# A searched table of steps: loads, transposes, dummies and output queues of a fused attention and gMLP kernel set in a new order

## The chip, the cores and the metric

The kernel runs on one core of a Trainium2 chip. The metric is the device time of one execution in microseconds (us). Engines are named as the profile names them: PE is the matrix engine (PEld its weight loads), DVE the vector engine, ACT the scalar engine, POOL GpSimd, SP the engine that issues most of the DMAs.

## The reference

One row of conditioning `c` is turned into six vectors, and these modulate a linear attention (hedgehog features, 16 heads of 28) and a gMLP with a 2048 x 2048 spatial matrix, over x of 2048 rows x 448.

```python
mod = (silu(c) @ w_mod)            # sa, ca, ga, sb, cb, gb, 448 each
# stage A
h = layernorm(x) * (1 + ca) + sa
q, k, v = split(h @ wqkv)          # 16 heads of 28
phi_q = concat(softmax(q @ w_phi), softmax(-q @ w_phi))
phi_k = concat(softmax(k @ w_phi), softmax(-k @ w_phi))
kv = sum_s phi_k^T v ;  z = sum_s phi_k
o = (phi_q @ kv) / (phi_q . z + 1e-6)
x = x + ga * (o @ wo)
# stage B
h = layernorm(x) * (1 + cb) + sb
z1, z2 = split(gelu(h @ w_in))     # 896 each
g = w_sp @ layernorm(z2) + b_sp    # w_sp 2048 x 2048, over the rows
x = x + gb * ((z1 * g) @ w_out)
```

## The kernel before

The 2048 rows are 16 tiles of 128, numbered 0 to 15. The work is cut into some 970 steps, and the string `ORDER` (lines 482 to 535) is the program: `fast_path` walks its words one after the other and issues what each names. Every engine runs its own instructions in that order and waits, by semaphores, for what it needs; nothing is reordered at run time. A word reads like this:

```python
kM:14@3      # step kM of tile 14, result in PSUM bank 3
kP:14/V      # step kP of tile 14, on DVE (/S is ACT, /G POOL, /Y SP)
ld:wout/Y    # load of w_out, issued by SP
T1:14,16     # DMA transpose of tiles 14 and 15, always on SP
```

The steps that the change and the prediction speak of, in order of the program:

- **Start.** `du:n` (L734) is n dummy matmuls on a zero tile, with no result. `ct` (L745) turns the row c; `FT`/`ET` (L824, L828) transpose the raw q and k weights, `PF`/`EP` (L840, L828) fold w_phi into them; `csA`/`ccA`, `csB`/`ccB` (L769) make the modulation vectors of stage A and stage B; `SH` (L783) and `SC` put them into the weights. `X:0` to `X:3` (L871) transpose the first four tiles of layernormed x on PE.
- **Stage 1, the keys.** Tiles 4 to 15 of layernormed x are transposed by DMA, two tiles a time: `T1:a,b` (issued at L863, `f_hT<-f_xpad`). Then, per tile, `kM` (L881) projects the keys, `kE`/`kF` (L884) take the exponentials on ACT, `kS` (L895), `kR` (L899) and `kP` (L902) normalise them, `vM` (L889) and `vC` project the values, and `kA` (L912) adds the tile to the sums kv, 8 small matmuls in one PSUM slot for all 16 tiles. `qM:0` to `qM:7` (L929) with `qE`/`qF` make the query features, each for four tiles and half of the heads. `gr:0` (L940) needs the load `wmga` and makes the gate ga, `gr:1` needs `wmgb` and makes gb. `kA:15` ends stage 1; `KV` copies the sums.
- **Stage 2, attention out and the input of the MLP.** `nM` (L957) multiplies query features by the sums, `nC`, `nS`, `nV`, `nT`, `nA` divide (`nT` is L976, on DVE), `T2` (L863, `f_oo<-f_oo`) transposes by DMA, `wM` (L992) multiplies by wo; `wN` is `wM` with one more matmul (L990) that adds x on PE. `wR`, `wQ`, `l2r`, `l2a` are the second layernorm, `T3` (L1032, `f_hT<-f_xpad`) its DMA transpose. `zM` (L1038) and `yM` (L1068) are the two halves of h @ w_in. `W:t,u` (L1076) loads an eighth of a quarter of w_sp by DMA transpose, 256 KB.
- **Spatial product and output.** `pM` (L1148) multiplies by w_sp, `oM` (L1097) by w_out, `oE` (L1113) adds to x, `oD` (L1116) stores a tile. Tile 15 is done in two halves, `oH`, `oG`, `oF` (L1102, L1106, L1110).

The loads go to SP in the order of their words (L655 to L686), with the transposes T1, T2, T3 and W between them, so one queue carries nearly all transfers. A DMA takes one of eight semaphores in turn, so the issue of a DMA on a queue waits for the landing of the one eight places earlier that used it. A function `general_path` stands behind a flag and isn't run with these inputs.

Of the kernel before, what the change touches and what calls it, by code (L numbers as in the profile page):

```python
# [486 lines left out]
SCq:2/S SCq:3/S SCq:0/S scb l1a:2/G X:2@6 XE:2/V ld:wv/Y ld:x4/Y SHv@2 SCv:2/V SCv:3/V l1e:4,8/G l1r:4,8 l1a:4/G SCv:0/S l1a:6/G kM:0@4 kM:1@7 kF:1
l1a:5/G SCv:1/S kE:1 kE:0 kF:0 kM:2@5 qM:0@A1 kE:2 qF:0 qE:0 ld:wmga/Y l1s:8 l1s:10 l1s:9 gr:0@0 ld:x5/Y ld:wo/Y kF:2 ge:0 vM:3@6 vM:1@4 vC:1 W:0,0
l1a:7/G m4 T1:4,6 kS:1 ld:wmgb/Y l1s:11 kS:0 kR:1 l1e:8,12/G kR:0 l1s:13 kP:1/G l1r:8,12 l1a:11/G T1:6,8 vM:0@7 l1s:12 kP:0/V kS:2 kR:2 W:0,5
ld:win1/Y l1a:9/G vM:2@3 vC:2 vC:0 l1s:14 l1s:15 l1e:12,16/G kM:3@5 kE:3 vC:3 l1r:12,16 l1a:15/G l1a:8/V T1:8,10 l1a:10/G kP:2/V T1:10,12 kM:5@2  # L490
kM:4@3 l1a:12/G l1a:14/G m6 kF:3 ld:wsb/Y T1:14,16 wos:3/V kS:3 kA:0@A0 l1a:13/G T1:12,14 kF:4 kR:3 kP:3/V kF:5 kE:5 kS:5 kE:4 W:0,3 W:0,6 kS:4 kR:4
vM:4@4 qM:1@C qF:1 kM:6@5 kF:6 kE:6 qM:2@A1 kS:6 qE:1 kP:4/V kR:5 qF:2 vM:5@5 vC:4 kA:1@A0 vC:5 kA:2@A0 kA:3@A0 qE:2 kM:7@7 kE:7 kF:7 ld:wcb/Y
ld:win0/Y wos:2/G kR:6 kP:5/V vM:7@4 vC:7 kS:7 kR:7 kP:7/V kM:8@6 kF:8 kE:8 kS:8 gr:1@7 W:0,4 kP:6/G kR:8 vM:6@5 kM:9@2 kE:9 kM:11@4 kF:9 kM:10@6 ge:1
kS:9 wos:1/G kR:9 kA:4@A0 kA:5@A0 vC:6 kA:6@A0 kE:11 kA:7@A0 kE:10 kF:10 kF:11 kS:11 kP:8/G kS:10 kR:10 kP:10/V vM:8@5 vC:8 vM:9@4 vC:9 kM:12@2 kE:12
kF:12 kA:8@A0 kM:14@3 kM:13@5 kP:9/G kE:13 kR:11 kP:11/G kS:12 kR:12 kF:13 ld:wout/Y kS:13 kR:13 kE:14 W:0,2 kM:15@7 kF:14 vM:10@2 vC:10 kA:9@A0 kF:15
kE:15 vM:13@6 vC:13 W:0,1 kP:12/V kS:14 kA:10@A0 vM:11@4 vC:11 vM:12@7 vC:12 vM:14@2 vC:14 kP:13/G kA:11@A0 kA:12@A0 vM:15@5 vC:15 kS:15 kR:15
kA:13@A0 kR:14 kP:14/V kA:14@A0 wts:1/G kP:15/V kA:15@A0 KV:1 qM:3@C qE:3 KV:0 csB@3 esB ccB@4 ecB nM:0@A1 nX:0 qF:3 nC:0 YB@1 YE W:0,7 nM:1@A2
wos:0/G wts:5/G wts:4/G SCw:1,0/G nX:1 nC:1 nS:0 nV:0 nT:0 nA:0/G T2:0,1 nT:1 nA:1/V T2:1,2 SCw:2,0/S SHw:2@0 SCw:0,2/S qM:4@C qF:4 nM:2@A0 nX:2
SHw:3@3 SCw:0,3/V nC:2 SCw:3,1/G qE:4 nM:3@A2 nX:3 SCw:2,1/S SCw:1,1/S qM:5@A1 qE:5 nM:4@C W:1,1 nC:3 nS:1 nV:1 nT:3 nT:2 nM:5@A2 nX:5 wN:0@0 nC:5
wN:1@1 nX:4 nC:4 nS:2 qF:5 wR:0/S wts:0/G wR:1/S nA:2/V nA:3/G T2:2,4 nV:2 nT:5 nA:5/G nT:4 W:1,3 nM:7@A1 nX:7 nC:7 wQ:0/S nM:6@A2 nX:6 qM:6@A0 wQ:1/S  # L500
lA:0,2/G lB:0,2/G lC:0,2/G lD:0,2/G SCw:3,0/S qF:6 nA:4/V T2:4,6 nC:6 nS:3 nV:3 nT:6 W:1,7 qE:6 wM:3@6 wN:2@7 wR:2/S l2r:0,2 l2a:1/G T3:1,2 nT:7
wR:3/V wQ:3/S qM:7@A2 qE:7 qF:7 nA:7/V l2a:0/G lA:2,4/G lB:2,4/G T3:0,1 wM:4@7 wQ:2/V lC:2,4/V lD:2,4/V l2r:2,4 l2a:2/G wR:4/V nA:6/V T2:6,8 l2a:3/G
# [803 lines left out]
```

## Time and profile before

| what | value |
| --- | --- |
| median of 3 runs | 250.22 us (249.93 to 250.77) |
| the profiled execution | 250.54 us, its span 248.7 us |
| mean granted PE clock | 0.995 |
| PE busy | 239.2 us, 96% of the span |
| DVE busy | 187.5 us, 75% |
| ACT busy | 115.7 us, 47% |
| POOL busy | 128.3 us, 52% |
| DMA, mean over the span | 25.23 MB, 101 GB/s |

Times in the views are counted from the start of the span. "Busy" of PE counts pipelined matmuls whose ends are modelled, so 96% says that PE has nearly no gap, not that it is at its peak. A row of a timeline gives start, length, engine, line, operation, output and inputs, count, and in brackets the idle time just before it with what ended it. Rows of SP in a timeline are the issue of a DMA, and that includes the time in which SP waited for room in the ring of semaphores; the time to landing is in the rows of the DMA view.

### The profile page before, as it was taken

What the parts mean: (1) busy time and instruction counts of PE and PEld (TensorE: products, weight loads), DVE (VectorE), ACT (ScalarE), POOL (GpSimd) and SP (SyncE); (2) the same over time, 40 slices, a digit from 0 to 9 for tenths busy, and PEclk for the clock granted to TensorE, in tenths of its full rate; (3) what the DMA queues carried; (4) which work ended last, traced back from release to release, by engine and by line L of the source; (5) the groups of instructions that cost most, each with busy time, mean ns of one, the idle gap of its engine ahead of it and who ended that gap; (6) DMA issues with size and microseconds to landing.
All of it is one profiled execution on the core that took longest, in us unless ns stands there. A gap on an engine that the chain in (4) does not pass through costs nothing.

```text
span 248.7 us, 4220 instructions
## 1 busy us (share of the span) xinstructions
PE 239.2 (96%) x1520; PEld 127.2 (51%) x1528; DVE 187.5 (75%) x374; ACT 115.7 (47%) x231; POOL 128.3 (52%) x172
## 2 busy tenths in 40 slices
PE   8899999999889999999999999999999999999992
PEld 6755566566535555544444444444444544444652
DVE  2889998977988988967357985858899754727652
ACT  3999887738889888787878110000010000000000
POOL 4768878576678556747855449601541901401000
PEclk9999999999999999999999999999999999999998
DMA  7998989970595634782100960009930120000022
GB/s 190 307 279 166 206 171 234 204 191 0 100 167 115 128 88 86 168 154 60 42 0 4 152 102 0 3 0 155 187 79 3 55 74 0 3 0 3 18 78 86
DMA packets 68800, 25.23 MB, mean 101 GB/s; under 512 B 58401, under 2 KB 68642, under 8 KB 68770
## 3 DMA queue, kind: packets, MB, share of 16 engines
q1 hardware_dynamic: 68160, 24.41, 48.9%
q10 hardware_dynamic: 610, 0.46, 0.6%
q8 instruction: 14, 0.23, 0.4%
q14 instruction: 16, 0.13, 0.2%
HBM read 8.87 MB, written 1.84 MB: 43 GB/s over the span
## 4 chain that ended last, share of the span: by engine, by line
PE 81%; DVE 10%; ACT 4%; DMA 2%; issue 1%; DVEq 0%; ACTq 0%; SPq 0%
PE f_psum L1148 29%; PE f_psum L1068 10%; PE f_psum L1038 9%; PE f_psum L1097 8%; PE f_psum L1084 6%; PE f_psum L992 4%; PE f_psum L929 3%; PE f_psum L881 3%; DVE f_ksum L895 2%; PE f_psum L889 2%; DVE f_t L976 2%; DMA f_oo<-f_oo 2%; PE f_psum L734 2%; DVE f_phik L902 1%; PE f_psum L957 1%; PE f_psum L783 1%
## 5 line engine op out<-in xcount | busy, mean ns | idle before, releaser
L1148 PEld LDWEIGHTS <-f_z2n 128*128 128x128 bf16 x192 | 18.7, 98 | 22.4
L1148 PE MATMUL f_psum<-f_wsp,f_z2n 128*128 128x512 bf16 x119 | 27.1, 379 | 0.1
L1068 PE MATMUL f_psum<-f_hT,f_win 112*128 112x512 bf16 x112 | 26.3, 379 | 0.0
L1038 PE MATMUL f_psum<-f_win,f_hT 112*128 112x448 bf16 (+1 forms) x128 | 26.1, 352 | 0.0
L1148 PE MATMUL f_psum<-f_hT,f_Eq 128*128 128x512 bf16 x92 | 22.3, 379 | 0.2
L1168 ACT COPY f_Eq<-f_psum 128x512 f32<-128x512 f32 x4 | 2.3, 586 | 40.0 <-PE f_psum L1148 40.0
L1097 PE MATMUL f_psum<-f_wout,f_z1T 128*128 128x448 bf16 x105 | 20.4, 352 | 0.0
L1071 ACT ACTIVATE f_z1T<-f_psum,f_yb 128x512 bf16<-128x512 f32 x28 | 17.8, 686 | 3.3 <-PE f_psum L1068 3.3
L934 ACT ACTIVATE f_Eq<-f_psum 112x1024 bf16<-112x1024 f32 x16 | 16.1, 1037 | 5.1 <-PE f_psum L929 5.1
L1038 PEld LDWEIGHTS <-f_hT 112*128 112x128 bf16 (+1 forms) x128 | 12.3, 97 | 11.7 <-DVE f_t L976 0.2
L1200 POOL TENSOR_TENSOR f_z1T<-f_gb,f_z1T 128x512 bf16<-128x512 f32 x6 | 7.8, 1310 | 19.3 <-DVE f_gb L1175 19.3
L976 DVE TENSOR_TENSOR f_t<-f_psum,f_w 128x896 bf16<-128x896 f32 x16 | 16.9, 1086 | 0.5
L895 DVE TENSOR_REDUCE f_ksum<-f_E 128x32 f32<-128x896 bf16 x16 | 16.8, 1066 | 0.6 <-ACT f_E L884 0.5
L1068 PEld LDWEIGHTS <-f_win 112*128 112x128 bf16 x112 | 10.9, 98 | 12.2
L884 ACT ACTIVATE f_E<-f_psum 128x448 bf16<-128x448 f32 x32 | 15.7, 565 | 2.6 <-PE f_psum L881 2.5
L1042 ACT ACTIVATE f_z2g<-f_psum 128x896 bf16<-128x896 f32 x16 | 14.6, 915 | 4.9 <-PE f_psum L1038 3.5
L929 PE MATMUL f_psum<-f_hT,f_Wq 113*128 113x512 bf16 (+1 forms) x64 | 15.2, 378 | 0.0
L1148 PEld LDWEIGHTS <-f_Eq 128*128 128x128 bf16 x96 | 9.4, 98 | 11.3
L992 PE MATMUL f_psum<-f_win,f_oo 112*128 112x448 bf16 x64 | 14.1, 352 | 1.1 <-DMA f_oo<-f_oo 0.9
L1097 PEld LDWEIGHTS <-f_z1T 128*128 128x128 bf16 x105 | 10.2, 98 | 9.4
L1113 DVE TENSOR_TENSOR f_xpad<-f_psum,f_x 128x448 bf16<-128x448 f32 x15 | 9.0, 618 | 7.5 <-PE f_psum L1097 7.5
L1175 DVE TENSOR_TENSOR f_z2g<-f_psum,f_z2g 128x512 f32<-128x512 f32 x12 | 8.3, 688 | 8.4 <-PE f_psum L1148 8.0
(214 smaller groups left out, 513.5 us busy)
## 6 DMA issues: line engine op xcount, KB each, us to landing
out_dram<-f_xpad SPq DMA_DIRECT2D x15, 112.0 KB, 1.7
f_wm<-in_w_mod_dram SPq DMA_DIRECT2D x4, 406.0 KB, 5.0
f_win<-in_B_w_in_dram SPq DMA_DIRECT2D x2, 784.0 KB, 6.6
f_x<-in_A_x_dram SPq DMA_DIRECT2D x3, 448.0 KB, 8.3
f_wmg<-in_w_mod_dram SPq DMA_DIRECT2D x2, 392.0 KB, 7.2
f_wout<-in_B_w_out_dram SPq DMA_DIRECT2D x1, 784.0 KB, 9.2
f_bsp<-in_B_b_sp_dram SPq DMA_DIRECT2D x1, 512.0 KB
f_wq_raw<-in_A_wqkv_dram ACTq DMA_DIRECT2D x1, 392.0 KB, 3.9
```

The costliest lines, as they stand in the source:

```text
L884: nc.scalar.activation(out=Er[i % NR][:, s, :], in_=ps["k" + str(i)][:, 0, 0:D], func=ACT.Exp, scale=1.0 - 2.0 * s)
L895: nc.vector.tensor_reduce(out=ksum[:, i], in_=Er[i % NR][:].rearrange("p s (c f h) -> p (s c) h f", c=4, h=HP), axis=AX.X, op=ALU.add)
L929: nc.tensor.matmul(t[:, u, :], lhsT=Wq[0:KR[m], m, cc * CB:cc * CB + P], rhs=hT[0:KR[m], 4 * st:4 * st + 4, m, :], start=(m == 0), stop=(m ...
L934: nc.scalar.activation(out=Eq[st // 2][0:CB, 2 * c2:2 * c2 + 2, s, (st % 2) * 512:(st % 2 + 1) * 512], in_=ps["q" + str(n)][0:CB, :, :], f ...
L976: nc.vector.tensor_tensor(out=tr[i % 2][:], in0=numv(i)[:, :, :, 0:DH], in1=wr[i // 2 % 2][:, i % 2].unsqueeze(3).to_broadcast([P, 2, H, D ...
L992: nc.tensor.matmul(t[:, 0, 0:D], lhsT=oT[0:CB, i % 4, cc, :], rhs=wo_s[0:CB, cc, :], start=(cc == 0 and not with_x), stop=(cc == KC - 1))
L1038: nc.tensor.matmul(t[:, hf, 0:D], lhsT=hT[0:KR[m], i, m, :], rhs=win_s[0:KR[m], m, FH + hf * D:FH + (hf + 1) * D], start=(m == 0), stop=(m ...
L1068: nc.tensor.matmul(t[:, 0, :], lhsT=win_s[0:CB, m, fc * P:(fc + 1) * P], rhs=hT[0:CB, 4 * st:4 * st + 4, m, :], start=(m == 0), stop=(m == ...
L1071: nc.scalar.activation(out=stage_b()["z1T"][:, fc, st * 512:(st + 1) * 512], in_=ps["y%d_%d" % (st, fc)][:, 0, :], func=ACT.Gelu_apprx_tan ...
L1084: nc.tensor.matmul(g[:, 0, 0:b - a], lhsT=later["z2n"][:, s_, fc * P:(fc + 1) * P], rhs=wspT[t][:, s_, a:b], start=(s_ == 0), stop=(s_ == ...
L1097: nc.tensor.matmul(ps["o" + str(t)][:, 0, 0:D], lhsT=later["z1T"][:, fc, t * P:(t + 1) * P], rhs=wout_s[:, fc, :], start=(fc == 0), stop=( ...
L1148: nc.tensor.matmul(t[:, 0, :], lhsT=b[:, j, f * P:(f + 1) * P], rhs=a[:, j, :], start=(PSTART[k] and j == 0), stop=(j == NH - 1), skip_gro ...
```

## The change

Only the string `ORDER` differs; no step has new code. The table has 975 words in place of 973:

- The dummies are 9, then five groups of 3 (24 matmuls), in place of 18, 3, 6 and 6 (33).
- The loads at the start stand in another order: on SP x0, phi, wk, x1 in place of x1, wk, phi, x2, x0; on ACT's queue c ahead of wq.
- Behind the first twelve loads of SP, the loads, the transposes T1 and the W loads are mixed in another order (below).
- `wN:2` is `wM:2`: the matmul that adds x in tile 2 goes (tiles 0 and 1 keep it), and DVE adds x there.
- Some 80 steps run on another engine than before (`kP` of 0, 1, 6 and others between POOL and DVE, `EP`, `SC`, `wQ` and `nA` between ACT, DVE and POOL).
- PE's own steps stand in another order within stages 1 and 2 and the start.
- Outputs: `oD` of tiles 1, 7, 8, 13 and 14 are issued by ACT in place of SP; of the two halves of tile 15 one changes from SP to ACT and the other from ACT to SP: `oF:15,0` is on ACT now, `oF:15,1` on SP.

Two lines of the string, the first words and the last:

```diff
-ld:wq/S m3 m2b/G m1/V m2a/G du:18@0 du:3@5 ld:c/S ct@2 tbl ce:1 ce:2 m5 ld:x1/Y l1s:1 ce:3 l1e:1,2/V l1r:1,2 l1a:1/G FTq:1@5 ETq:1/S FTq:0@6 ETq:0/S
+du:9@2 ld:x0/Y l1s:0 m1/V m5 du:3@3 ld:c/S ct@0 du:3@3 ld:wq/S FTq:1@5 m2a/G m2b/G l1e:0,1/G l1r:0,1 l1a:0/G m4 tbl ce:1 ce:2 ce:3 ce:4 ld:phi/Y bd/V
...
-oM:12,0,7@3 oE:12 oM:13,0,7@2 oE:13 oD:7/Y oD:10/Y oD:11/Y oD:9/Y oD:13/Y oD:12/Y oM:14,0,7@1 oE:14 oD:14/Y oH:15,0@5 oG:15,0 oF:15,0/Y oH:15,1@6
-oG:15,1 oF:15,1/S hint
+oM:12,0,7@3 oM:13,0,7@2 oE:13 oD:13/S oD:2/Y oE:12 oD:12/Y oE:10 oD:11/Y oD:10/Y oM:14,0,7@1 oE:14 oD:14/S oH:15,0@5 oG:15,0 oF:15,0/S oH:15,1@6
+oG:15,1 hint oF:15,1/Y
```

**SP in stage 1.** Before, these rows stand on SP behind the loads of x and of wo (L863 into `f_hT` is T1, L1076 is W, L681 the load wmgb, L662 the loads wsb and then wcb, L655 into `f_win` from `in_B_w_in` is win1 and then win0):

```order
L1076 DMA_TRANSPOSE f_wsp_84<-in_B_w_sp_dram 128x8x128
L863 DMA_TRANSPOSE f_hT<-f_xpad 128x8x128
L681 DMA f_wmg<-in_w_mod_dram 112x4x448
L863 DMA_TRANSPOSE f_hT<-f_xpad 128x8x128
L1076 DMA_TRANSPOSE f_wsp_84<-in_B_w_sp_dram 128x8x128
L655 DMA f_win<-in_B_w_in_dram 112x4x896
L863 DMA_TRANSPOSE f_hT<-f_xpad 128x8x128 x2
L662 DMA f_wm_120<-in_w_mod_dram 112x4x464
L863 DMA_TRANSPOSE f_hT<-f_xpad 128x8x128 x2
```

After, these rows stand behind the loads of x (L685 is wout, L655 from `in_A_wo` is wo, L686 is bsp; of the six T1 the first is T1:4,6, then T1:6,8 and T1:10,12, then T1:8,10 and T1:12,14, the last T1:14,16):

```order
L1076 DMA_TRANSPOSE f_wsp_84<-in_B_w_sp_dram 128x8x128
L685 DMA f_wout<-in_B_w_out_dram 128x7x448
L863 DMA_TRANSPOSE f_hT<-f_xpad 128x8x128
L655 DMA f_win<-in_A_wo_dram 112x4x448
L681 DMA f_wmg<-in_w_mod_dram 112x4x448
L662 DMA f_wm_120<-in_w_mod_dram 112x4x464
L863 DMA_TRANSPOSE f_hT<-f_xpad 128x8x128 x2
L1076 DMA_TRANSPOSE f_wsp_84<-in_B_w_sp_dram 128x8x128 x3
L863 DMA_TRANSPOSE f_hT<-f_xpad 128x8x128 x2
L1076 DMA_TRANSPOSE f_wsp_84<-in_B_w_sp_dram 128x8x128
L662 DMA f_wm_120<-in_w_mod_dram 112x4x464
L1076 DMA_TRANSPOSE f_wsp_84<-in_B_w_sp_dram 128x8x128
```

and directly behind them:

```order
L655 DMA f_win<-in_B_w_in_dram 112x4x896
L686 DMA f_bsp<-in_B_b_sp_dram 128x2048
L863 DMA_TRANSPOSE f_hT<-f_xpad 128x8x128
L1076 DMA_TRANSPOSE f_wsp_84<-in_B_w_sp_dram 128x8x128
L655 DMA f_win<-in_B_w_in_dram 112x4x896
```

Before, two W and one half of w_in stood ahead of the T1:14,16 (the first of the last pair, T1:12,14 is the second). After, T1:14,16 is the last of the six and stands behind six W, wout, one half of w_in, both L662 loads and bsp, which before stood behind T3:10,12, deep in stage 2.

**PE behind the first three tiles of keys.** Before, the queries of the first four tiles (L929) follow:

```order
L881 MATMUL f_psum<-f_Wk,f_hT 128x448
L881 LDWEIGHTS f_hT
L881 MATMUL f_psum<-f_Wk,f_hT 128x448
L929 LDWEIGHTS f_Wq
L929 MATMUL f_psum<-f_hT,f_Wq 128x512
```

After, the gate's matmuls (L940, `gr:0`) follow at that place, and `qM:0` comes behind three `vM`:

```order
L881 MATMUL f_psum<-f_Wk,f_hT 128x448
L881 LDWEIGHTS f_hT
L881 MATMUL f_psum<-f_Wk,f_hT 128x448
L940 LDWEIGHTS f_scb
L940 MATMUL f_psum<-f_wmg,f_scb 128x448
```

So `gr:0` stands 8 matmuls of 512 columns earlier than before.

**Outputs on SP.** The rows at the end of SP's program before (L1218 reads the flag of the general path):

```order
L1116 DMA out_dram<-f_xpad 128x448 x8
L1218 TENSOR_LOAD flag
L1218 ISA x2
L1116 DMA out_dram<-f_xpad 128x448 x7
L1110 DMA out_dram<-f_xpad 128x224
```

and after:

```order
L1116 DMA out_dram<-f_xpad 128x448 x6
L1218 TENSOR_LOAD flag
L1218 ISA x2
L1116 DMA out_dram<-f_xpad 128x448 x4
L1110 DMA out_dram<-f_xpad 128x224
```

Five full outputs and the first half of tile 15 are issued by ACT now, and the second half, the last, by SP.

More of the change, by code (lines that the diff above doesn't have):

```diff
@@ L487 @@
[L487 to L502, printed above, removed]
@@ L535 @@
+cA:1,1,12 cX:1,1,12/V gG:2,6 oM:8,0,7@3 oE:8 oD:8/S oM:9,0,7@2 oE:9 oD:9/Y cX:1,1,22/V gM:4,6@6 oM:10,0,7@0 gG:3,6 gG:4,6 read oM:11,0,7@4 oE:11
+oM:12,0,7@3 oM:13,0,7@2 oE:13 oD:13/S oD:2/Y oE:12 oD:12/Y oE:10 oD:11/Y oD:10/Y oM:14,0,7@1 oE:14 oD:14/S oH:15,0@5 oG:15,0 oF:15,0/S oH:15,1@6
+oG:15,1 hint oF:15,1/Y
 """
```

81 lines of the change are left out of this document (48 added, 33 removed).

## The prediction

> **What bounds the kernel now.** I read the page first: its busy times, its slices, its chain.
>
> ```profile
> span 248.7 us, 4220 instructions
> PE 239.2 (96%) x1520; PEld 127.2 (51%) x1528; DVE 187.5 (75%) x374; ACT 115.7 (47%) x231; POOL 128.3 (52%) x172
> PE   8899999999889999999999999999999999999992
> DMA  7998989970595634782100960009930120000022
> ```
>
> PE is busy for 239.2 us of 248.7, and its row has only nines behind the second slice, but for slices 11 and 12 (62 to 75 us) and the last. So the time is the start of steady PE work, plus PE's work, plus what it waits, plus the tail. The second thing to see is the DMA row: 7 to 9 tenths in the first nine slices, up to 56 us. The transfers of stage 1 are nearly as full as PE there, and they feed it. PE's timeline gives the start of the steady part, the end of stage 1 and all later waits:
>
> ```profile
> 15.55 2.45 PE L881 MATMUL f_psum<-f_Wk,f_hT 113*128 113x448 bf16 x12
> 53.59 1.90 PE L929 MATMUL f_psum<-f_hT,f_Wq 113*128 113x512 bf16 x8
> 64.74 0.59 PE L957 MATMUL f_psum<-f_KVbd,f_Eq 112*128 112x120 bf16 x8 [0.67 <-DVE f_t L976]
> 65.73 0.35 PE L990 MATMUL f_psum<-f_x,f_ident 128*128 128x448 bf16 x1 [0.40 <-DVE f_t L976]
> 71.38 0.93 PE L992 MATMUL f_psum<-f_win,f_oo 112*128 112x448 bf16 x4 [0.89 <-DMA f_oo<-f_oo]
> 80.58 1.67 PE L992 MATMUL f_psum<-f_win,f_oo 112*128 112x448 bf16 x8 [0.20 <-DVE f_t L976]
> ```
>
> The first keys (kM) start at 15.55; `kA:15` has ended and `qM:3` starts at 53.59. Call that point K. Between them no row shows a wait. The four waits in stage 2 add up to 2.16 us, and that is all there is to be gained behind the start, except for the tail.
>
> **The main term: T1:14,16.** The last transpose of layernormed x is now issued behind much more. Before:
>
> ```profile
> 33.17 3.68 SPq L863 DMA_TRANSPOSE f_hT<-f_xpad  x2
> f_hT<-f_xpad SPq DMA_TRANSPOSE x1, 5.3
> 42.32 0.58 SPq L685 DMA_DIRECT2D f_wout<-in_B_w_out_dram  x1
> f_wout<-in_B_w_out_dram SPq DMA_DIRECT2D x1, 784.0 KB, 9.2
> f_win<-in_B_w_in_dram SPq DMA_DIRECT2D x2, 784.0 KB, 6.6
> f_bsp<-in_B_b_sp_dram SPq DMA_DIRECT2D x1, 512.0 KB
> ```
>
> The first row's first transfer is T1:14,16; the second row is its time from issue to landing, so it landed at 33.17 + 5.3 = 38.5. Where will it land? I count what stands ahead of it in the new order: behind the loads of x these are wo, wmgb, wsb, wcb, win1, wout, bsp, six W and the other five T1. Compare what before had issued when it came to wout, at 42.32: the same loads without bsp and with win0, five W, and six T1. A W is 128x8x128 in bf16, 256 KB, and so is a T1. The new set, with T1:14,16 itself, has one W and bsp more (768 KB) and one half of w_in less (784 KB): equal to 16 KB. Before, that set had landed with wout, at 42.32 + 9.2 = 51.5. So with the queue as full as before, T1:14,16 would land at 51.5 in place of 38.5.
>
> The queue can be fuller, since before it had holes:
>
> ```profile
> 6.00:18.00 12.00, 11.09 (x140) 8.26 (x138) 10.70 (x35) 11.55 (x22) 8.14 (x14) 1.00 1.14 303
> 18.00:22.00 4.00, 4.00 (x22) 1.95 (x20) 3.83 (x9) 4.00 (x8) 3.10 (x9) 1.00 1.19 103
> 30.00:35.00 5.00, 5.00 (x45) 3.10 (x44) 4.97 (x7) 5.00 (x10) 4.56 (x8) 1.00 0.63 109
> 35.00:46.70 11.70, 11.70 (x94) 7.04 (x93) 10.69 (x19) 8.59 (x20) 7.92 (x5) 1.00 1.13 237
> ```
>
> The last column is GB/s. Full, with loads and transposes mixed, it moved 237. In 18 to 22 it moved 103, so 4 x (1 - 103/237) = 2.3 us went unused; in 30 to 35, 5 x (1 - 109/237) = 2.7. In the new order wout stands in the first hole, where SP waited for tiles 4 and 5 of layernormed x. All 5.0 recovered gives 46.5, none gives 51.5; new holes at transposes that wait for x can open too. I take 3.2 of the 5.0, so 48.3.
>
> When does PE need it? Prices of its steps, from the chain of waits:
>
> ```profile
> 33.24 0.76 PE f_psum L881 x4
> 34.00 0.76 PE f_psum L889 x4
> 29.50 1.74 PE f_psum L929 x8
> 25.82 0.42 PE f_psum L912 x8
> 55.49 0.78 PE f_psum L769 x32
> ```
>
> In the new order, from its first kM to `kM:14`, stand 14 kM, 12 vM and 2 gates (28 x 0.76 = 21.3), 3 qM (5.2) and 10 kA (4.2): 30.7 us. From 15.5 that is 46.2. So PE waits 2.1 there. From `kM:14` to the end of `kA:15` stand 2 kM, 4 vM, 6 kA and csB (half of the last row), 7.5 us, and DVE and POOL have kS, kR and kP of the last two tiles to do meanwhile. K becomes 48.3 + 0.1 + 7.5 = 55.9 in place of 53.59: **+2.3** (0 to +5.5 for landings of 46.2 to 51.5; the first 7.7 us of the delay, 38.5 to 46.2, cost nothing). An earlier wait costs nothing beside it: T1:6,8 stands behind wout and wsb now (1.2 MB, some 5 us at 237) and may keep `kM:7` 1 to 2 us, but then `kM:14` is reached later and its wait is shorter by as much.
>
> [...]
>
> **The start.**
>
> ```profile
> 1.23 3.85 PE L734 MATMUL f_psum<-f_zero 128*128 128x256 bf16 x21 [1.23 <-DVE f_zero L695]
> 6.17 0.82 PE L734 MATMUL f_psum<-f_zero 128*128 128x256 bf16 x6
> f_wmg<-in_w_mod_dram SPq DMA_DIRECT2D x1, 392.0 KB, 10.6
> 7.05 1.20 SPq L680 DMA_DIRECT2D f_wmg<-in_w_mod_dram  x1
> ```
>
> The dummies fill time in which PE waits for the first weights, so nine fewer take nothing off by themselves. The weights' chain through ACT is one step shorter (an `EP` on DVE); the first kM can be up to 0.5 earlier. But `gr:0` now follows the first three kM, near 17.3, and its load landed at 7.05 + 10.6 = 17.6, so PE waits there for 0.3 to 0.8. Together **0** (-0.5 to +0.8).
>
> **Stage 2.** The matmul that adds x in tile 2 goes (about 0.2 where it is not at a gap, and DVE adds x as for other tiles), and csB moves ahead of K (about 0.4, counted there). Its waits have other places: T2 now stands behind fewer loads but between other W, and `nT` on DVE (L976) still paces `nM`. I can't read from the trace which of the four waits go; I see new places of equal size (`yM:0,0` behind T3:2,4, `zM:11` right behind `zM:12` in one PSUM slot). All four gone would be -2.2 and new ones of their size +2.2. As the nearest rows are the present waits themselves, I take about their sum again and a little more for the new places: **+0.4** (-1.5 to +1.5). Where DVE, ACT and POOL swap steps, about as many come to each engine as leave it; with PE the bound at 96% I take 0.
>
> **From 136 us on** PE's order differs little, and nothing there waits before or need wait now: 0. bsp used to be loaded in stage 2 and is not waited for there.
>
> **The tail.**
>
> ```profile
> 240.00 5.02 SPq L1116 DMA_DIRECT2D out_dram<-f_xpad  x6
> 244.13 0.39 DVE L1106 TENSOR_TENSOR f_xpad<-f_psum,f_x 128x224 bf16<-128x224 f32 x1 [0.28 <-PE f_psum L1102]
> 244.55 0.38 ACTq L1110 DMA_DIRECT2D out_dram<-f_xpad  x1
> 245.12 0.71 SPq L1110 DMA_DIRECT2D out_dram<-f_xpad  x1
> out_dram<-f_xpad SPq DMA_DIRECT2D x1, 56.0 KB, 2.1
> ```
>
> The first half of tile 15 was ready at about 243.9, but SP was still issuing full tiles until 245.02, so it went out at 245.12 and landed last, at 247.2. Now ACT issues it and five of the tiles, and SP is free when the second half is ready, 244.55: **-0.6** (0 to -0.6).
>
> The sum: 0 + 2.3 + 0.4 - 0.6 = +2.1 on the profiled execution's 250.54, 252.64. That execution lies 0.3 above the median of 250.22, so I predict 250.22 + 2.1 = 252.3. A measurement of this kernel can tell about 0.3%, 0.75 us, from no change.
>
> **The rivals.**
>
> Loads keep up, faster. If the queue moves more, as the 303 GB/s of 6 to 18 us (13.0 us of extra queue would be 13.0 x 237/303 = 10.2, landing 48.7 with the holes and under 46.2 with half of them closed), or all holes close, T1:14,16 lands by about 46.2 and the main term is 0 or below: with PE at its first kM 0.5 earlier and the tail's 0.6, the sum is -0.6 to -1.6, about 249.2. For it: the holes are real, 5.0 us. Against it: closing them all is just enough, and any wait of SP for a tile of x opens another. Chance 0.20.
>
> No change: the wait at `kM:14` is about 0.6 and the tail pays for it, or stage 2's waits go. 250.3, chance 0.14.
>
> PE's clock, slower by another cause. With 9 dummies in place of 18 first, and single groups of 3 behind, PE is idle more between 2 and 6 us.
>
> ```profile
> L734 PE MATMUL f_psum<-f_zero x33: 270/273/421, 1.2 to 8.7; 128*128 128x256 bf16 x33
> ```
>
> The 21 first took 3.85 us, 0.18 each from start to start, and the 6 later 0.82, under 0.14: PE speeds up in this stretch. If it comes up late, the matmuls of 6 to 13 us, of which PE does some 5 us, take up to a third longer: at most +1.5, and 251.5 if the loads keep up. It decides when PE is on the path ahead of 15.5; mostly it waits for ACT and loads there. [...] By it nine dummies would not do; the later matmuls would, since they follow closely, so I leave its chance at 0.06.
>
> The forecast has the rest, 0.60; most of the clock's case counts as slower too.
>
> **The range.** The forecast's own is 251 to 255 (landings of 47.0 to 51.0). To hold eight in ten it reaches down into the case in which the loads keep up, to 249.6, and up to 254.6. Faster by over 0.3%: 0.20. Within: 0.14. Slower: 0.66.
>
> **What would show it.** In the profile after: an idle time of PE of about 2 us ahead of `kM:14` (L881) put down to the transpose into f_hT; K near 55.9; wout in flight at 20 us; the last half tile issued by SP as soon as DVE has made it. If K is below 53.6, the main term is wrong. If K is late without a wait on the transpose, DVE's or POOL's share of kS, kR, kP is the cause, which I have set at nothing. If PE starts kM after 16, the start is mis-sized.

## The result: slower by 2.3%, and the profile after

The changed kernel took 256.94 us (median of 255.31 to 257.35), the kernel before 250.5: a ratio of 1.023, 95% interval 1.020 to 1.026. The prediction was 252.3 with a range up to 254.6: the sign was right, the size was not. The profiled execution took 257.35 us.

The page after, in the parts shown of before (span, busy times, PE's slices, granted clock, DMA):

```profile
span 255.6 us, 4215 instructions
PE 241.4 (94%) x1518; PEld 126.5 (49%) x1518; DVE 189.6 (74%) x378; ACT 117.2 (46%) x234; POOL 120.4 (47%) x165
PE   5799998989989999999999999999999999999990
PEclk9979999999999999999999999999999999999998
DMA  6999999990177936433010790001950011000112
```

PE's first two slices have 5 and 7 in place of 8 and 8, and the third slice has a granted clock of 0.7. PE's timeline after, with its waits at the start and in stage 1 (idle time in brackets), and K, the queries behind kA:15:

```profile
6.30 1.03 PE L824 MATMUL f_psum<-f_ident,f_wq_raw 112*112 112x112 bf16 x16 [1.40 <-DMA f_wq_raw<-in_A_wqkv_dram]
12.57 0.55 PE L769 MATMUL f_psum<-f_scol,f_wm 112*128 112x1 bf16 x16 [1.18 <-DMA f_wm<-in_w_mod_dram]
14.70 1.66 PE L783 MATMUL f_psum<-f_Wk,f_Ga 112*128 112x448 bf16 x4
18.85 2.45 PE L881 MATMUL f_psum<-f_Wk,f_hT 113*128 113x448 bf16 x12
39.39 1.69 PE L881 MATMUL f_psum<-f_Wk,f_hT 113*128 113x448 bf16 x8 [0.57 <-DMA f_hT<-f_xpad]
41.45 0.59 PE L912 MATMUL f_psum<-f_vaug,f_phik 128*128 128x116 bf16 x8 [0.36 <-POOL f_phik L902]
52.08 0.93 PE L881 MATMUL f_psum<-f_Wk,f_hT 113*128 113x448 bf16 x4 [0.81 <-DMA f_hT<-f_xpad]
59.55 1.90 PE L929 MATMUL f_psum<-f_hT,f_Wq 113*128 113x512 bf16 x8
```

The first kM starts 3.3 us later than before (18.85 against 15.55). K is at 59.55 against 53.59. The wait ahead of `kM:14` is there (52.08), 0.81 us long. The four stretches, from the timelines of both profiles:

| stretch | before | after | difference | predicted |
| --- | --- | --- | --- | --- |
| span's start to first kM | 15.55 | 18.85 | +3.30 | 0 |
| first kM to K | 38.04 | 40.70 | +2.66 | +2.3 |
| K to the spatial product (L1084) | 82.56 | 81.73 | -0.83 | +0.4 |
| from there to the end of the span | 112.55 | 114.32 | +1.77 | -0.6 |
| sum | 248.7 | 255.6 | +6.9 | +2.1 |

In the last stretch the way to the end of DVE's last instruction is as long as before (108.3 and 108.4); what grew is the tail behind it, 4.21 before and 5.91 after. Below, "stage 1" is the second row and "tail" this time.

### The profile page after: what moved, and what is told of

It reads as the page before. It is cut to its first block, busy times and chain, and to the rows that moved or that the text cites. A ratio compares the mean times of both kernels' runs of the same rounds, so it can differ in the third digit from the quotient of the medians.

```text
span 255.6 us, 4215 instructions
## 1 busy us (share of the span) xinstructions
PE 241.4 (94%) x1518; PEld 126.5 (49%) x1518; DVE 189.6 (74%) x378; ACT 117.2 (46%) x234; POOL 120.4 (47%) x165
## 3 DMA queue, kind: packets, MB, share of 16 engines
q10 hardware_dynamic: 1330, 1.03, 1.3%
## 4 chain that ended last, share of the span: by engine, by line
PE 76%; DVE 10%; DMA 7%; POOL 2%; SPq 1%; issue 1%; ACT 0%; POOLq 0%; DVEq 0%; ACTq 0%
PE f_psum L1148 28%; PE f_psum L1038 10%; PE f_psum L1068 9%; PE f_psum L1097 8%; PE f_psum L1084 5%; PE f_psum L992 4%; DMA f_wm<-in_w_mod_dram 4%; DMA f_hT<-f_xpad 4%; PE f_psum L929 3%; PE f_psum L957 2%; DVE f_ksum L895 2%; DVE f_st L847 2%; PE f_psum L783 1%; DVE f_t L976 1%; POOL f_phik L902 1%; DVE f_xpad L858 1%
## 5 line engine op out<-in xcount | busy, mean ns | idle before, releaser
L895 DVE TENSOR_REDUCE f_ksum<-f_E 128x32 f32<-128x896 bf16 x16 | 16.7, 1054 | 0.3 <-ACT f_E L884 0.2
L881 PE MATMUL f_psum<-f_Wk,f_hT 113*128 113x448 bf16 (+1 forms) x64 | 14.1, 352 | 1.5 <-DMA f_hT<-f_xpad 1.4
L929 PE MATMUL f_psum<-f_hT,f_Wq 113*128 113x512 bf16 (+1 forms) x64 | 15.2, 379 | 0.0
L902 POOL TENSOR_TENSOR f_phik<-f_E,f_kr 128x896 bf16<-128x896 bf16 x7 | 11.9, 1708 | 4.9 <-DVE f_kr L899 4.3
```

The lines of the kernel that those rows point to most:

```text
L895: nc.vector.tensor_reduce(out=ksum[:, i], in_=Er[i % NR][:].rearrange("p s (c f h) -> p (s c) h f", c=4, h=HP), axis=AX.X, op=ALU.add)
L902: eng.tensor_tensor(out=pr[i % NR][:, 0:2 * D].rearrange("p (a f h) -> p a f h", a=8, h=HP), in0=Er[i % NR][:].rearrange("p s (c f h) -> p ...
L929: nc.tensor.matmul(t[:, u, :], lhsT=Wq[0:KR[m], m, cc * CB:cc * CB + P], rhs=hT[0:KR[m], 4 * st:4 * st + 4, m, :], start=(m == 0), stop=(m ...
```

## Experiments

Each kernel was timed beside the kernel before, on the same chip; the chip was not the same for all of them. The medians of before were 250.9 to 251.1 there, and across chips the ratio to before is the safer figure.

**The changed kernel again.** No edit.

> The changed kernel once more, unaltered. If the late start (first kM at 18.85 us, the second modulation load landing at 14.2 at 245 GB/s, half clock from 14 to 18 us) belongs to the kernel, its profile shows a first kM near 18.8 again and a time of 256 to 257. If it was the chance of one execution, the first kM is at 15.5 to 16.5 and the time nearer 254.

255.5 us (254.27 to 257.62). First kM at 16.79, stage 1 40.99, tail 5.61. So about 2 of the 3.3 us of the first profile's start come and go from run to run; 1.2 stay here. (In the kernel before, three profiles with its start unchanged have the first kM at 15.55, 15.92 and 16.19.) The 254.3 to 257.6 of this kernel is wider than the 250.3 to 252.3 of before beside it. 255.5 is the base of what follows.

A length of stage 1 comes from one profile each. With the change's stage 1 unaltered it was 39.90 to 41.60 in seven profiles (these two and five further down), and 37.74 to 38.04 in four with the stage 1 of before. So two single profiles that differ by less than 1.7 there show nothing by themselves; PE's waits, with what ended them, show more.

**The start's loads.**

```diff
-du:9@2 ld:x0/Y ... ld:c/S ... ld:wq/S ... ld:phi/Y bd/V ld:wk/Y
+du:9@2 ld:x0/Y ... ld:wq/S ld:c/S ... ld:wk/Y ld:phi/Y bd/V
```

> Only the start's loads: wq ahead of c on ACT's queue, wk ahead of phi on SP, as before. Theory: the start is late because the loads that the weights wait for come later; then wq lands at 4.7 in place of 6.25, the second modulation load near 12, the first kM is at 16 to 16.5, and the time falls by 2 to 3. Rival: the missing first dummies let PE fall to half clock and the loads don't matter; then wq lands early, but the two L783 groups still take 1.66 and the time falls by under 1.

253.82 us, ratio to before 1.0101 (1.0075 to 1.0128), where the changed kernel beside it had 1.0179 (1.0138 to 1.0219). The gain of 1.7 is less than the expected 2 to 3, and more than the rival's 1. With 252.91 to 254.27 its times lie closer together, too. First kM at 16.18, and the weights' matmuls (L783) at 0.92, with a granted clock of 1.00 from 12 to 18 us:

```profile
13.69 0.92 PE L783 MATMUL f_psum<-f_Wk,f_Ga 112*128 112x448 bf16 x4
16.18 2.45 PE L881 MATMUL f_psum<-f_Wk,f_hT 113*128 113x448 bf16 x12
```

The repetition of the changed kernel has L783 at 0.92 too, so these rows do not part the two readings; the times do.

**The dummies.**

```diff
-du:9@2
+du:18@2
```

> Only the first dummies: 18 in place of 9 (33 in all, as before). Theory of the loads: PE waits at 5 to 6 and at 11 to 14 us for loads whatever ran before, so the first kM stays at 18 to 19 and the time within 0.5. Theory of the dummies: PE keeps its clock, the two L783 groups take 0.92 each in place of 1.66, and the time falls by 1.5 to 2.

256.89 us (254.86 to 257.98): no gain, and three of its six times near 258. The profiled run was the fastest of the six (254.86), and it did what the theory of the dummies said: L783 took 0.92 and the first kM came at 15.81. The first 16 transposes of the raw weights took 0.99 in it; in the repetition of the changed kernel, with nine dummies, 1.74. The row of the repetition, then of this run:

```profile
5.86 1.74 PE L824 MATMUL f_psum<-f_ident,f_wq_raw 112*112 112x112 bf16 x16 [0.67 <-DMA f_wq_raw<-in_A_wqkv_dram]
```

```profile
6.55 0.99 PE L824 MATMUL f_psum<-f_ident,f_wq_raw 112*112 112x112 bf16 x16
```

So these 16 matmuls were faster behind 18 dummies (0.99 against 1.74), but the time as a whole says that the dummies do not cure the loss. What happened in the three executions near 258 is not known, since none of them was profiled.

**The same two parts, put into the kernel before.**

```diff
-ld:wq/S ... ld:c/S ... ld:wk/Y ... ld:phi/Y
+ld:c/S ld:wq/S ... ld:phi/Y ld:wk/Y
```

> The kernel before with only two swaps in the start's loads: c ahead of wq on ACT's queue, phi ahead of wk on SP. Theory of the loads: wq lands a little over 1 us later than 4.6, the first kM comes at 16 to 17 in place of 15.55, and the time rises by 0.8 to 1.8. Rival: the start is bound by ACT's chain of copies, and the time stays within 0.5.

251.26 us, ratio 1.0002 (0.9985 to 1.0019). The first kM moved to 16.93, as the theory said, but the spatial product starts at 136.38 against 136.15: the waits of stage 2 took up all of the lateness. The expected loss did not come.

```diff
-du:18@0
+du:9@0
```

> The kernel before with 9 first dummies in place of 18 and nothing else. Theory of the loads: PE waits for wq until 4.6 anyway, and the time stays within 0.5. Theory of the dummies: the matmuls of the weights run at half clock, the first kM comes 0.5 to 1.5 later and the time rises by as much.

250.88 us, ratio 0.9979 (0.9961 to 0.9996). Nine dummies fewer cost nothing in the time of the kernel before; if anything they gain 0.2%, less than I count as a difference. In the profile, though, the start is what the theory of the dummies said: the first kM at 16.73, 1.2 later than in the profile of before, and the first transposes at 1.75 in place of 1.03. The row of before, then of this run:

```profile
5.30 1.03 PE L824 MATMUL f_psum<-f_ident,f_wq_raw 112*112 112x112 bf16 x16
```

```profile
5.19 1.75 PE L824 MATMUL f_psum<-f_ident,f_wq_raw 112*112 112x112 bf16 x16
```

The spatial product starts at 135.98 in spite of it, so stage 2 took up this lateness as well.

So in the kernel before neither part alone costs time, since stage 2 has about 1 us of waits to give. In the changed kernel the load order costs 1.7.

**The transposes.** T1:8,10 and T1:14,16 forward on SP:

```diff
-T1:10,12 W:0,0 ... W:0,6 W:0,1 ... T1:8,10 ... T1:12,14 ... W:0,4 ... ld:wcb/Y W:0,7 ... ld:win1/Y ... ld:bsp/Y ... T1:14,16
+T1:10,12 T1:8,10 W:0,0 ... W:0,6 ... T1:12,14 T1:14,16 W:0,1 ... W:0,4 ... ld:wcb/Y W:0,7 ... ld:win1/Y ... ld:bsp/Y
```

> The changed kernel with two transposes of x brought forward on SP: T1:8,10 directly behind T1:10,12, and T1:14,16 directly behind T1:12,14; three W, wcb, win1 and bsp now stand behind them. Theory of the queue: T1:14,16 lands near 42, no wait for the transposes is left, stage 1 (first kM to the queries behind kA:15) falls from 40.7 to 41.0 to about 38.5 (38.0 as before plus 0.4 for the modulation matmuls that now stand in it), and the time falls by 1.5 to 2.5 against the changed kernel's 255.5. Rival: DVE, ACT and POOL, which share the key steps in another way now, hold PE in the same stretch; then the waits on the transposes go but stage 1 stays at 40 or more and the time falls by less than 1.

254.73 us, 0.8 less (ratio to before 1.0128, 1.0109 to 1.0148; the changed kernel 1.0179, 1.0138 to 1.0219: the intervals overlap). No wait for a transpose is left, but stage 1 is 40.22: the rival held. DVE's timeline of this run shows what holds it, with POOL's below:

```profile
34.92 0.35 DVE L899 RECIPROCAL f_kr<-f_ksum 128x32 bf16<-128x32 f32 x1 [0.84 <-POOL f_phik L902]
35.19 3.24 DVE L946 TENSOR_TENSOR f_win<-f_win,f_g_rep 112x448 bf16<-112x448 bf16 x1
```

```profile
33.20 4.98 POOL L902 TENSOR_TENSOR f_phik<-f_E,f_kr 128x896 bf16<-128x896 bf16 x3
38.14 2.17 POOL L946 TENSOR_TENSOR f_wout<-f_wout,f_g_rep 128x448 bf16<-128x448 bf16 x2
```

DVE's second row is `wos:3`, 112x448, which took 0.38 in the kernel before. It ends at 38.43, 0.25 behind POOL's third kP, while POOL goes on without a gap to 40.31. The profile of the changed kernel has the same in another place, `l1a:13`; DVE first, then POOL:

```profile
33.16 3.20 DVE L858 TENSOR_SCALAR f_xpad<-f_x,f_nm,f_rs 128x448 bf16<-128x448 bf16 x1
36.28 1.07 DVE L895 TENSOR_REDUCE f_ksum<-f_E 128x32 f32<-128x896 bf16 x1
```

```profile
32.47 1.40 POOL L946 TENSOR_TENSOR f_win<-f_win,f_g_rep 112x448 bf16<-112x448 bf16 x1
33.86 0.71 POOL L858 TENSOR_SCALAR f_xpad<-f_x,f_nm,f_rs 128x448 bf16<-128x448 bf16 x1
34.54 1.69 POOL L902 TENSOR_TENSOR f_phik<-f_E,f_kr 128x896 bf16<-128x896 bf16 x1
37.91 3.48 POOL L902 TENSOR_TENSOR f_phik<-f_E,f_kr 128x896 bf16<-128x896 bf16 x2 [1.68 <-DVE f_kr L899]
```

DVE's instruction begins while POOL is in a run of three without a gap, and ends at 36.36, when POOL's run has ended at 36.23.

**One step more, to POOL.**

```diff
 (with the transposes forward)
-wos:3/V
+wos:3/G
```

> The kernel of the run with the earlier transposes (T1:8,10 and T1:14,16 forward), and one step more moved: wos:3, the multiplication of a part of wo by the gate, from DVE to POOL. There it took 3.24 us on DVE, 35.2 to 38.4, while POOL ran three kP without a gap (33.2 to 38.2); alone it takes 0.38. Theory: the two engines exclude each other for such instructions, DVE stands still for 2.9 us and with it the keys' chain; then no DVE instruction of this kind takes over 1 us there, stage 1 falls from 40.2 to 38.0 to 38.8, and the time falls by 0.7 to 1.5 against 254.7. Rival: DVE simply has more to do between 24 and 57 us; then stage 1 falls by 0.4 or less and POOL's kP come later.

253.46 us (252.87 to 257.09), ratio 1.0097 (1.0063 to 1.0131), which overlaps with that of the run before it. Its profiled run, at 257.09, was the slowest of its six, with a first kM at 18.54. Stage 1 took 39.61 in it, and the standstill was there again, at the other instruction: `l1a:13` on DVE, 3.19 us. The time fell by 1.3, as expected but not clear of the noise; the standstill didn't go.

**The same cost, put into the kernel before.** `wos:3` from its quiet place to one where POOL runs kP:

```diff
-ld:wsb/Y T1:14,16 wos:3/V
+... ge:1 kS:9 wos:3/V wos:1/G
```

> The kernel before with one DVE step put later: wos:3 behind kS:9, where POOL runs kP of two tiles without a gap, in place of 28.0 us where POOL ran nothing between two tiles of x. Theory of the exclusion: this instruction, 0.38 before, takes 1 to 3 us and ends when POOL's second kP ends. Rival: it was slow in the changed kernel for another reason (a semaphore, a busy memory), and takes 0.4 to 0.8 here. The time changes by less than 1, since stage 2 of before takes up about a microsecond of lateness.

251.24 us, ratio 1.0014 (0.9992 to 1.0037). DVE's row, and POOL's:

```profile
41.01 1.44 DVE L946 TENSOR_TENSOR f_win<-f_win,f_g_rep 112x448 bf16<-112x448 bf16 x1
```

```profile
40.51 1.69 POOL L902 TENSOR_TENSOR f_phik<-f_E,f_kr 128x896 bf16<-128x896 bf16 x1 [0.92 <-PE f_psum L912]
42.88 1.69 POOL L902 TENSOR_TENSOR f_phik<-f_E,f_kr 128x896 bf16<-128x896 bf16 x1 [0.68 <-DVE f_kr L899]
```

1.44 in place of 0.38, and its end, 42.45, lies 0.25 behind that of POOL's kP. Here POOL had a gap behind one kP, and DVE came through in it. That is the standstill, made on purpose, 1.06 us of it. It cost nothing here: stage 1 was 37.74.

**Both small steps to POOL, without and with the earlier transposes.**

```diff
-l1a:13/V ... wos:3/V
+l1a:13/G ... wos:3/G
```

> The changed kernel with only wos:3 and l1a:13 on POOL, the transposes late as in the change. By the prediction's main term T1:14,16 still lands near 50 and PE waits for it 1 to 2.5 us, so stage 1 is 1 to 2.5 longer than in the run with the transposes forward, 39.5 to 41. Rival: the late transposes hid behind DVE's standstill or the other way round; then either alone keeps stage 1 near 40, and only both together bring it to 38.5.

255.67 us: no gain. Stage 1 40.13, in the expected 39.5 to 41, where the rival and the unaltered changed kernel lie as well; the wait for the transposes, in the list of PE's waits, is 1.2 us and the only one left in stage 1:

```profile
PE f_psum L881 <- DMA f_hT<-f_xpad: 1.2, 1, 1.2
```

> The changed kernel with the two transposes forward and both wos:3 and l1a:13 on POOL. Theory of the exclusion: no DVE instruction of stage 1 takes over 2 us, and stage 1 falls from 40.2 to 38.0 to 38.8; the time 253 or less. Rival: the keys' chain on DVE and POOL is slower by its new split; stage 1 stays at 39.3 or more.

254.14 us, and stage 1 41.81, longer still; the expectation was missed. (The profiled execution took 256.56; six of the eight took 253.2 to 254.7.) The standstill had moved to a third instruction, a kP of 0.6 us on DVE. DVE first, POOL below it:

```profile
37.78 4.61 DVE L902 TENSOR_TENSOR f_phik<-f_E,f_kr 128x896 bf16<-128x896 bf16 x1
```

```profile
33.95 4.98 POOL L902 TENSOR_TENSOR f_phik<-f_E,f_kr 128x896 bf16<-128x896 bf16 x3
38.89 1.03 POOL L946 TENSOR_TENSOR f_win<-f_win,f_g_rep 112x448 bf16<-112x448 bf16 x1
39.88 2.03 POOL L946 TENSOR_TENSOR f_wout<-f_wout,f_g_rep 128x448 bf16<-128x448 bf16 x2
```

POOL runs from 33.95 to 41.91 without a gap; DVE's kP stands from 37.78 to 42.39. So no single DVE step is the cause: three of them, `wos:3` (3.24), `l1a:13` (3.20) and this kP (4.61), stood still where POOL had a run of instructions without a gap. With more steps given to POOL the run got longer. How many of POOL's instructions a DVE instruction waits for is not the same each time: here it was the rest of one and three more, to the end of the run; `wos:3` above waited for the rest of one kP and one more, and came in though POOL went on.

**The run broken.** The same kernel with the middle one of the three kP back on DVE, where it was before the change:

```diff
 (with the transposes forward, l1a:13/G and wos:3/G)
-kP:2/G ... kP:5/G ... kP:4/G
+kP:2/G ... kP:5/V ... kP:4/G
```

> The changed kernel with the two transposes forward, wos:3 and l1a:13 on POOL, and kP:5, the middle one of POOL's three kP in a row, back on DVE. Theory: POOL then has a gap, no DVE instruction of stage 1 takes over 2 us, stage 1 falls from 41.8 to 38.2 to 39.2 and the time from 254.1 to 252 to 253. Rival: DVE, with one kP more, is the bound; stage 1 stays at 39.8 or more.

Stage 1 fell from 41.81 to 38.43, as expected, PE's timeline shows no wait in it, and no kP on DVE takes over 1.8 us (count, then shortest, median and longest in ns):

```profile
L902 DVE TENSOR_TENSOR f_phik<-f_E,f_kr x10: 618/822/1802, 28.3 to 55.5; 128x896 bf16<-128x896 bf16 x10
```

The time did not fall with it (254.39, expected 252 to 253; 254.14 without this edit), so in the time this step shows no gain. This profile has a late start again, first kM at 18.21, and a tail of 6.31, both of which this kernel keeps from the change. The late start may have shortened stage 1 too, since the transfers and POOL had more time ahead of PE; how much of the fall is due to it isn't known.

**The tail.** First DVE's order alone. This kernel stores tile 10's rows in the place of tile 2 too, so its output of tile 2 is another.

```diff
-oE:11 oM:12 oM:13 oE:13 oD:13/S oD:2/Y oE:12 oD:12/Y oE:10 oD:11/Y oD:10/Y
+oE:11 oE:10 oM:12 oM:13 oE:12 oE:13 oD:13/S oD:2/Y oD:12/Y oD:11/Y oD:10/Y
```

> Only DVE's order of the last full tiles is changed: oE:10 and oE:12 ahead of oE:13 again, the queues as in the changed kernel. Theory: the outputs bunch because oE:12 and oE:10 stand behind oE:13; then the stretch from the last DVE instruction to the end of the span falls from 6.0 to 4.2 us or less, and the time by 1.5 to 2. Rival: the second output queue itself makes the late stores slow; then the stretch stays at 5.5 to 6 and the time does not move.

254.78 us, 0.7 less, and a tail of 5.61, the rival's. The last half was issued at once and landed 2.5 us later, but the span went on to 253.1.

Then the queues as before and DVE's order as before, with the stores' order of the change (13, 12, 11, 10) left on SP:

```diff
-oE:11 ... oE:13 ... oE:12 ... oE:10
+oE:11 ... oE:10 ... oE:12 ... oE:13
-oD:1/S oD:8/S oD:13/S oD:14/S oF:15,0/S hint oF:15,1/Y
+oD:1/Y oD:8/Y oD:13/Y oD:14/Y oF:15,0/Y oF:15,1/S hint
```

> The changed kernel with the tail of before: SP issues all outputs but the last half tile, which ACT issues, DVE adds tiles 10, 12, 13 in order of their matmuls, and the branch hint stands last. Theory: the tail, from the end of DVE's last instruction to the end of the span, is 4.2 in place of 5.6 to 5.9, and the time falls by 1.4 against the changed kernel's 255.5. Rival: the tail depends on the run; it stays above 5 and the time within 0.5.

255.2 us and a tail of 6.41: no gain. I had taken this for the tail of before, and it wasn't: on SP the stores of 12, 11 and 10 stood behind that of 13, and none went out from 240.4 to 244.9.

With the stores in the order of the tiles as well:

```diff
-oE:13 oD:13/S oD:2/Y oE:12 oD:12/Y oE:10 oD:11/Y oD:10/Y
+oD:2/Y ... oE:11 oE:10 ... oE:12 ... oE:13 oD:10/Y oD:11/Y oD:12/Y oD:13/Y
```

> The changed kernel with only the tail replaced: DVE adds and SP stores tiles 8 to 14 in the order in which their matmuls end, ACT stores the last half, the hint last. Theory: the tail was long because the stores of tiles 10, 11 and 12 stand behind that of 13; then the tail is 4.2 to 4.6 and the time falls by 1.2 to 1.8 against 255.5. Rival: it stays above 5.3 whatever the order, and the time within 0.5.

253.87 us, ratio 1.0115 (1.0079 to 1.0151), and a tail of 4.31: 1.6 less, as expected. Over all profiles the tail parts the kernels cleanly: 5.4 to 6.4 us in the twelve with one of the two orders of the change left (DVE's adds out of order, or the stores of 12, 11 and 10 in falling order), 4.0 to 4.7 in the eight with neither. The end of the timeline, of the changed kernel and then of this one (rows of SPq and ACTq are the issues of stores):

```profile
246.59 2.21 DVE L1113 TENSOR_TENSOR f_xpad<-f_psum,f_x 128x448 bf16<-128x448 f32 x4 [2.02 <-PE f_psum L1097]
249.25 0.39 DVE L1106 TENSOR_TENSOR f_xpad<-f_psum,f_x 128x224 bf16<-128x224 f32 x1 [0.15 <-PE f_psum L1102]
250.35 0.81 SPq L1110 DMA_DIRECT2D out_dram<-f_xpad  x1
```

```profile
246.15 0.62 DVE L1113 TENSOR_TENSOR f_xpad<-f_psum,f_x 128x448 bf16<-128x448 f32 x1 [0.70 <-PE f_psum L1097]
247.49 0.39 DVE L1106 TENSOR_TENSOR f_xpad<-f_psum,f_x 128x224 bf16<-128x224 f32 x1 [0.28 <-PE f_psum L1102]
247.91 0.38 ACTq L1110 DMA_DIRECT2D out_dram<-f_xpad  x1
```

In the changed kernel DVE waits 2.02 us for the matmuls of tile 13 and then does four tiles in a row, so their stores come at once, and the last half is issued 0.71 behind DVE's end; its landing, in the DMA view, takes 3.7 us. In the other it is issued 0.03 behind and takes 2.5:

```profile
out_dram<-f_xpad SPq DMA_DIRECT2D x1, 56.0 KB, 3.7
```

```profile
out_dram<-f_xpad ACTq DMA_DIRECT2D x1, 56.0 KB, 2.5
```

**The two queues by themselves,** in the kernel before:

```diff
-oD:1/Y oD:8/Y oD:7/Y oD:13/Y oD:14/Y oF:15,0/Y oF:15,1/S
+oD:1/S oD:8/S oD:7/S oD:13/S oD:14/S oF:15,0/S oF:15,1/Y
```

> The kernel before with only the output queues of the change: tiles 1, 7, 8, 13, 14 and the first half of 15 on ACT, the second half on SP; DVE's order as before. By the prediction's step the last half goes out at once and the time falls by 0.6. Rival: two queues that store at the same time finish later, and the time is the same or up to 1.5 longer.

251.15 us, ratio 0.9994 (0.9971 to 1.0017). The last half was issued 0.25 us earlier than before (244.87 against 245.12), but took 3.1 us to land in place of 2.1:

```profile
out_dram<-f_xpad SPq DMA_DIRECT2D x1, 56.0 KB, 3.1
```

So the second queue brought nothing by itself. (In three other profiles with the queues and the order of before, the store that SP issued last took 2.3 to 2.6 us.)

**Everything undone.** Four parts first: the start's loads, the transposes, `wos:3`, and the tail that wasn't yet that of before.

> All four undone at once in the changed kernel: wq ahead of c and wk ahead of phi at the start, the two transposes forward, wos:3 on POOL, the tail of before. If these four are the loss and add up, the time is that of before, 250.5 to 251.5. If something else of the change costs as well, it stays at 252 or more; if stage 2's new order is a gain by itself, it falls below 250.3.

253.76 us; stage 1 39.42 with `l1a:13` at 3.19, the tail 5.81. Then with both DVE steps on POOL and the stores in order:

> The changed kernel with five things undone: the loads' order at the start, the two transposes forward, both DVE steps (wos:3 and l1a:13) on POOL, and the tail with stores on SP in the order of the tiles. If these are the loss, stage 1 takes 38.0 to 38.8, the tail 4.2 to 4.6 and the time is 250.5 to 251.5, that of before. If something is left, it stays at 252 or more.

252.07 us, ratio 1.0044 (1.0023 to 1.0065), above the expected 250.5 to 251.5: something is left. Stage 1 38.79 with no wait of PE in it, the tail 4.01, no kP on DVE over 1.7. And with two of the three kP back on DVE:

```diff
 (the kernel above)
-kP:2/G ... kP:5/G
+kP:2/V ... kP:5/V
```

> The version with five things undone (252.1 us, stage 1 38.8), and kP:2 and kP:5 back on DVE as before. Theory: the rest of its difference to the kernel before is POOL's run of kP; stage 1 falls to 38.2 to 38.5 and the time to 250.8 to 251.6, equal to before. Rival: it stays at 252 and stage 2 or the start keeps the rest.

251.41 us, ratio 1.0013 (0.9993 to 1.0032): equal to the kernel before, as expected. Its rows of the span and of K:

```profile
span 249.9 us, 4213 instructions
```

```profile
54.28 1.90 PE L929 MATMUL f_psum<-f_hT,f_Wq 113*128 113x512 bf16 x8
```

Stage 1 was 38.85 there, not the expected 38.2 to 38.5 and not below the 38.79 of the step before it, so the last 0.7 us of the time can't be put down to these two steps by this profile, and the two intervals overlap. What is shown: the order of the start's loads, the late transposes, the steps that went between DVE and POOL and the order of the last stores together hold the whole loss. How it divides among them is shown for the loads (1.7) and the tail (1.6), and less surely for the other two. The rest of the new order, stage 2's and the nine dummies among it, neither costs nor gains anything that shows. No version beat the kernel before by more than about 0.2%.

## Why the prediction was wrong, step by step

**The main term, T1:14,16: right in kind, too large.** It was priced at +2.3, with a wait of 2.1 at `kM:14`. The wait is there in four of the eight profiles with the late transpose, 0.81, 1.16, 1.36 and 1.19 us (the changed kernel, its repetition, and the runs with only the tail or only the two POOL steps changed); in the other four PE, held up before, came after the landing. Where the transpose was moved forward no wait on one is left. The transpose landed at 52.0 in the first profile (the end of that wait), 3.7 later than priced, with a start 3.3 late; in the other three the wait ended at 49.1 to 50.3, with starts 0.9 to 1.2 late. An earlier wait, 0.57 for the tiles 8 and 9, came in the first profile as well. The two delays lie side by side in part, DVE's standstill and the wait: moved forward alone it gained 0.8, while the intervals overlap. That stage 1 as a whole came out at +2.66, near the +2.3 of this term, is luck: PE waited 1.4 for transposes there, and the rest has other causes.

**The swap of steps between DVE, ACT and POOL: priced at 0, and that failed.** "About as many come to each engine as leave it" counts busy time and says nothing of which instructions run beside which. POOL's runs of kP and its neighbours stopped a DVE instruction for 3.2 us in ten profiles, and the keys' chain with it. What that cost is read from PE's waits in stage 1. In the seven profiles with the change's stage 1 PE waited 0.4 to 1.7 us for transposes and 0.3 to 1.0 for the exponentials or the normalised features of the keys. With the transposes forward the second kind was 0.8 to 1.1 in the three profiles with a standstill of 3.2 us, 2.3 in the one with 4.61, and none in the three where no such DVE instruction took over 1.8. Without waits stage 1 took 38.4 to 38.9, 0.4 to 0.8 more than in the profile of before; csB, now ahead of K, is 0.4 of that. In the times this cause shows less: moving the two DVE steps alone gained nothing (255.67), nor did breaking POOL's run alone (254.39 against 254.14). So that the standstill holds the keys up is shown; how many microseconds of the loss are its own is argued from PE's waits.

**The start: priced at 0 (-0.5 to +0.8), measured +0.9 to +3.3** in the ten profiles with the change's loads and nine first dummies. I looked at the wait for wmga, which did not appear in the changed kernel (0.17 and 0.30 us in two of the later runs). What came was two things. One is c ahead of wq on ACT's queue and phi ahead of wk on SP's: PE waited 0.45 to 1.40 for wq in these ten profiles. The other is the step "nine fewer take nothing off by themselves", which failed in the profiles: the first transposes of the raw weights (L824, 16 of wq) took 0.99 to 1.17 us in all five profiles with 18 first dummies, and 1.70 to 1.75 in ten of the fifteen with nine. The granted clock shows none of it (a 9, nine tenths or more, in the first two slices of the PEclk row in all twenty); only the instructions' times do. In the first profile PE waited 1.40 for wq and 1.18 for the modulation weights, and then its clock fell. The windows of the changed kernel (the first figure with a count is PE's busy time; third from the end stands the granted clock, last the GB/s), then of before:

```profile
10.00:12.00 2.00, 1.18 (x19) 0.91 (x17) 1.72 (x5) 1.93 (x5) 1.73 (x5) 1.00 1.12 248
12.00:14.00 2.00, 1.43 (x32) 1.29 (x32) 1.64 (x6) 1.00 (x3) 1.89 (x4) 1.00 1.14 245
14.00:16.00 2.00, 1.75 (x21) 0.98 (x21) 1.07 (x4) 1.36 (x3) 0.85 (x3) 0.67 1.15 249
16.00:18.00 2.00, 2.00 (x9) 0.97 (x8) 1.30 (x4) 1.19 (x2) 0.19 (x1) 0.50 1.11 220
```

```profile
12.00:14.00 2.00, 1.70 (x27) 1.12 (x26) 1.41 (x4) 1.55 (x4) 1.54 (x3) 1.00 1.12 319
16.00:18.00 2.00, 2.00 (x12) 1.01 (x11) 1.93 (x6) 2.00 (x6) 1.85 (x3) 1.00 1.28 273
```

The clock is 0.67 and then 0.50 behind a stretch in which PE was busy for 2.6 of 4 us (1.18 and 1.43 in two windows of 2), and L783 takes 1.66 in place of 0.92. The rival of the clock was given 0.06 and tied to the dummies. Slow first matmuls with nine dummies are what it spoke of. How many dummies make PE's matmuls fast, on which the 0.06 leaned, no run shows: behind nine, L824 took 1.70 to 1.75 in ten profiles and 0.99 to 1.03 in five. The fall at 14 us is another thing, and what goes with it is idle time of PE: the clock fell in four of the twenty profiles (a 7 in the third slice of the PEclk row, where the other sixteen have a 9), all with the change's order of loads, and these are the four in which PE was busy for only 2.3 to 2.9 us of some stretch of 4 us between 8 and 14.5 us; in the other sixteen it was 3.1 or more. With wq and wk first again none of four profiles has the fall. That the late loads cause it is likely from this, not shown by a run of its own. That the loads moved 220 to 249 GB/s in this stretch, and 273 to 319 before, explains nothing yet: two other profiles with the change's loads, the repetition and the run with the transposes and both POOL steps, had 249 and 239 at 12 to 15 us at a granted clock of 1.00, with the first kM at 16.79 and 16.81.

**The tail: priced at -0.6, measured +1.7, the wrong sign.** The step "SP is free when the second half is ready" held in no run of the changed kernel: I looked at the queues alone and passed over DVE's order, in which tile 13 stands ahead of 12 and 10, and SP's, in which the stores follow it. And the gain that I took for the free queue is not there even where the queue is free: the store took 3.1 us in that run, 2.1 to 2.6 in four profiles with the queues of before.

**Stage 2: +0.4 priced, -0.83 measured;** about 0.4 of it is csB, counted at K. But the stretch from K to the spatial product took 81.5 to 82.9 in five profiles with the stage 2 of before and 81.7 to 82.9 in those with the new one, so neither the +0.4 nor a gain is shown. The waits of 0.2 to 0.9 there are waits with slack behind them, since a K up to 1.1 us later in the kernel before was taken up by the spatial product.

In sum, the miss is the start and the tail, which the prediction put at 0 and -0.6 and which measured +3.3 and +1.77 in the first profile. The steps that failed are the start's sum of 0, in which the new order of the loads was not weighed at all, the tail's free queue, and the swap of steps between engines at nothing; T1:14,16 was the right wait with too large a size.

## What to carry to other kernels

When a table of steps is searched anew, don't sum the busy time of the engines that swap steps: look where DVE's bf16 instructions on SBUF now meet an unbroken run of POOL's, since several of POOL's instructions in a row held one up for 3.2 and 4.61 us here. Follow the last outputs through every engine that they pass, from the order of the adds to the order of the stores, before counting a second queue. Count a late load at the start as a wait (1.40 and 1.18 us in the first profile), and look at the clock behind it, which was 0.50 there. Ask of each loss at the start what stands behind it, too: about a microsecond of it cost nothing in the kernel before (first kM 1.4 and 1.2 us later, 251.26 and 250.88 us).
